# A fused attention and MLP kernel: a decay scan in longer chunks, a smaller first key load, and three transfers and copies put elsewhere

## The chip, the cores and the metric

The kernel runs on one core of a Trainium2 chip. The metric is the device time of one execution in microseconds (us). Before the change it is 359.97 us, the median of three runs (359.89 to 360.4). The profile shows one execution with a span of 358.2 us; all positions in time below are counted from the start of that span.

## The reference

```python
def _attn_ref(q, k, v, s):              # 8 batches, 8 heads, 576 positions, 64 wide
    scores = scale * np.matmul(q, k.transpose(0, 1, 3, 2))
    s_pos = np.maximum(s, 0.0)
    cum = np.cumsum(s_pos, axis=-1)
    bias = -(cum[:, :, :, None] - cum[:, :, None, :])
    scores = np.where(causal, -1000000000.0, scores + np.minimum(bias, 0.0))
    scores = scores - np.max(scores, axis=-1, keepdims=True)
    attn = np.exp(scores)
    attn = attn / (np.sum(attn, axis=-1, keepdims=True) + 1e-09)
    return np.matmul(attn, v)

def _moe_ref(x, w_in, w_out):           # x: 4608 tokens of 512; w_in 512x2048, w_out 2048x512
    h = x @ w_in
    relu6 = np.clip(h + 3.0, 0.0, 6.0)
    return (h * relu6 / 6.0) @ w_out
```

Attention with a decay: each position has a number `s`, its positive part is summed along the sequence, and the difference of two such sums is taken from the score. The result of attention, with the heads side by side, is the input of an MLP with a hardswish between its two matrices.

## The kernel before

**Pairs of heads.** The 64 heads are worked in 32 pairs. A pair has 1152 rows of queries and keys, which are 9 tiles of 128. A tile is cast to f16 and transposed, so that `qT` and `kT` hold 64 rows of head width; four more rows (64 to 67) carry the decay. The running sum enters as three f16 parts of the key (`hi`, `mid`, `lo`, which add up to the f32 value) against rows of ones in the query, and as one negated part in the query against a row of ones in the key. In the other rows up to 127 there is a coarse causal mask. `qkT` has three slots for three pairs in turn.

**Four ways to fill those rows.** The first four pairs (`FIRST = 4`) and the fifth go through `x0`, a tile that lies in the second half of `gT2`: POOL (for a few parts of pair 0 ACT) casts q and k into it, and TensorE transposes its columns of 68 (`turn_first`). The decay columns of these five pairs (`COLS = 5`) are made at the very start by `first_columns`. Pairs 5 to 9 take the decay rows from a scratch tensor in DRAM (`load_aug`); later pairs are transposed by the DMA from `xb`, whose columns 64 to 127 hold mask constants: `load_columns` loads these constants (`xaug`, 288 KB) and `copy_columns` puts them into the two `xb` buffers, once each, on DVE.

**`first_columns`.** `s_first` holds 90 chunks of 64 values of `s`, one chunk to a partition. DVE scans each chunk. TensorE then turns the chunks to columns and adds what the chunks before hold, in f32: for each half of the 128 partitions one matmul with a selection matrix and one with a matrix of "chunks before" (both in `sums`, 63.3 KB of constants). From the result in PSUM DVE makes `hi`, ACT makes the negated column out of `hi`, and DVE makes the rest, `mid` and `lo`.

**Order of the work.** The order in which instructions are written is the order on each engine; there is no scheduler. What matters of it:

- The start: `s_first`, the first parts of q and k of pair 0 and all of pair 1 are put on the queues of SP and ACT; TensorE runs six matmuls on zeros (`keep_warm(6)`), ACT casts, `first_columns` follows, then the first transposes and the first scores. After them comes a loop over the eight heads of pairs 0 to 3, in which the transposes of the next pair stand between the two halves of a head's scores (`scores_half`). `cast_pair(3)` is in the loop at head 3, the transposes of its queries at head 4.
- POOL issues the four quarters of `w_in` (512 KB each as they arrive) at head 4, two before and two after a cast of v, and the four of `w_out` after the loop. A one-row copy out of `w_out_sb` (`fence_dram`) on SP's queue holds the loads of pair 4 back until the third quarter of `w_out` has landed.
- After the loop the MLP of the first 512 tokens begins (`m1`, then `m2`). In between, the decay of all later pairs is computed: `decay_scan`, `decay_rows`, `decay_columns`, and at last on POOL `decay_order`, twelve small copies and one multiplication by -1 into `dec` (L282). Then POOL casts q and k of pair 4 (`cast_pair(FIRST)`), while DVE makes both `copy_columns`. TensorE does four pieces of `m2` and then transposes pair 4.
- `second_pair` works pairs 4 to 8, with the transposes for the next pair and pieces of `m2` in between; after that `weave` mixes attention and MLP by their costs.

Of the kernel before, what the change touches and what calls it, by code (L numbers as in the profile page):

```python
# [9 lines left out]
F32 = mybir.dt.float32  # L10
# [6 lines left out]
def kernel(  # L17
# [48 lines left out]
    def pair_of_banks(b):  # L66
        return PS[:, b:b + 2, :].rearrange("p b c -> p (b c)")

    FIRST = 4
    COLS = FIRST + 1  # L70
    NG = COLS * W2 // 64
    g = np.arange(NG)
    sel_np = g[:, None] == g[None, :]
    low_np = (g[:, None] < g[None, :]) & (g[:, None] // 9 == g[None, :] // 9)
    sums_dram = nc.inline_tensor(
        np.ascontiguousarray(
            np.stack([m[:, k::2] for k in range(2) for m in (sel_np, low_np)], axis=1)
        ).astype(np.float32),
        name="sums",
    )  # L80

# [41 lines left out]
        "p (a t i c) -> p a t i c", a=COLS, t=NTR, i=2  # L123
    )

    s_first = work.tile([NG, 64], F32, tag="s_first", bufs=1)
    sums = work.tile([NG, 4, NG // 2], F32, tag="sums", bufs=1)
    scan = work.tile([NG, 64], F32, tag="scan", bufs=1)
    rest = work.tile([128, NG // 2], F32, tag="rest", bufs=1)
    s_sb = work.tile([NH, SEQ], F32, tag="s0", bufs=1)  # L130
    s8 = work.tile([NH, SEQ], F32, tag="s1", bufs=1)
    c8 = work.tile([NH, SEQ], F32, tag="s2", bufs=1)
# [57 lines left out]
    def mask_rows(sl, i):  # L190
        nc.vector.tensor_copy(out=mask_view(sl, i), in_=mask_view(0, i))
# [11 lines left out]
    def load_part(p, i, t0, t1, eng):  # L203
        b, h0 = (2 * p) // H, (2 * p) % H
        rows = (q, k)[i][b, h0:h0 + 2].rearrange("h s d -> (h s) d")
        eng.dma_start(  # L206
            out=qk_f[p][:, t0:t1, i, :],
            in_=rows.rearrange("(t p) d -> p t d", p=128)[:, t0:t1, :],
        )
# [98 lines left out]
    def transpose_group(p, g):  # L308
        t0, t1 = ((0, 5), (5, 9))[g]
        n = (t1 - t0) * 128  # L310
        pT = f16(PS[:, 3, :], n)
        src = qk_h[p]
        for t in range(t0, t1):
            c = (t - t0) * 128
            transpose_tile(pT[:, c:c + 128], src[:, t, :, :], t == t0, t == t1 - 1)
        sl = p % NS
        c0 = t0 * 128
        for dst, r0 in ((qT, 0), (kT, 64)):
            nc.vector.tensor_copy(out=dst[0:64, sl, c0:c0 + n], in_=pT[r0:r0 + 64, 0:n])  # L319
        if g == 1:  # L320
            qk_h.pop(p)
# [264 lines left out]
    def keep_warm(n):  # L586
        pw = PS[:, 3, :]
        for i in range(n):
            nc.tensor.matmul(
                out=pw, lhsT=warm[:, 0:128], rhs=warm, start=(i == 0), stop=(i == n - 1)  # L590
            )
# [56 lines left out]
    def second_pair(p, fill):  # L648
        s0, s1, v = scores(2 * p), scores(2 * p + 1), values(2 * p)
        first = p == FIRST  # L650

        def more(n=1):
            run(fill[:n])
            del fill[:n]

        load_pair(p + 3)
        run(s0[:1])
        if not first:
            transpose_group(p, 1)
        run(s0[1:2])  # L660
        if not first:
            run(values(2 * p - 1)[0])
        run(s0[2:3])
        if not first:
            run(values(2 * p - 1)[1])
        run(s0[3:])
        cast_qk(p + 1)
        more()
        run(s1[:2])
        if not first:  # L670
            x_transpose(p - 1)
        run(v[0] + s1[2:3] + v[1])
        if not first:
            transpose_group(p + 1, 0)
        run(s1[3:])
        if first:
            transpose_group(p + 1, 0)
        if p + 3 < PTD:
            load_aug(p + 3, nc.sync)
        cast_v(p + 1)  # L680
        if PTD <= p + 2:
            cast_columns(p + 2)
            transpose_dma(p + 2)
        more()
# [57 lines left out]
    def run(tasks):  # L742
        for task, _ in tasks:
            task()

    def first_columns():
        nc.vector.tensor_scalar(
            out=s_first, in0=s_first, scalar1=0.0, scalar2=8.0, op0=ALU.max, op1=ALU.mult
        )
        nc.vector.tensor_tensor_scan(  # L750
            out=scan, data0=s_first, data1=s_first, initial=0.0, op0=ALU.add, op1=ALU.max
        )
        key_rows()
        cT = PS[:, 7, 0:NG // 2]
        for half in range(2):
            o = cT[64 * half:64 * half + 64, :]
            nc.tensor.matmul(
                out=o, lhsT=scan, rhs=sums[:, 2 * half, :], start=True, stop=False
            )
            nc.tensor.matmul(  # L760
                out=o, lhsT=scan[:, 63:64].to_broadcast([NG, 64]), rhs=sums[:, 2 * half + 1, :],
                start=False, stop=True,
            )
        c3 = cT.rearrange("p (a t) -> p a t", a=COLS)
        r3 = rest.rearrange("p (a t) -> p a t", a=COLS)
        hi, mid, lo = (x0[:, :, :, 1, D + j] for j in range(3))
        nc.vector.tensor_copy(out=hi, in_=c3)
        nc.scalar.activation(out=x0[:, :, :, 0, D + 3], in_=hi, func=AF.Copy, scale=-1.0)
        nc.vector.tensor_tensor(out=r3, in0=c3, in1=hi, op=ALU.subtract)
        nc.vector.tensor_copy(out=mid, in_=r3)  # L770
        nc.vector.tensor_tensor(out=lo, in0=r3, in1=mid, op=ALU.subtract)

    def cast_first(p, i, t0, t1, copy):
        copy(out=x0[:, p, t0:t1, i, 0:D], in_=qk_f[p][:, t0:t1, i, :])  # L774

    def turn_first(p, i, t0, t1, b, copy):
        pT = f16(pair_of_banks(b) if (t1 - t0) > 8 else PS[:, b, :], (t1 - t0) * 128)
        for t in range(t0, t1):
            c = (t - t0) * 128
            nc.tensor.matmul(  # L780
                out=pT[0:XW, c:c + 128], lhsT=x0[:, p, t, i, :], rhs=ident,
                is_transpose=True, start=(c % 1024 == 0),
                stop=(t == t1 - 1 or c % 1024 == 896),
            )
        dst = (qT, kT)[i]
        copy(out=dst[0:XW, p % NS, t0 * 128:t1 * 128], in_=pT[0:XW, :])  # L786
# [1 line left out]
    V, A, G = nc.vector, nc.scalar, nc.gpsimd  # L788

    qk_tile(0)  # L790
    nc.sync.dma_start(out=s_first, in_=s.rearrange("b h (c t) -> (b h c) t", t=64)[0:NG])
    load_part(0, 0, 0, 5, A)
    A.dma_start(out=sums, in_=sums_dram.ap())
    load_part(0, 1, 0, 5, nc.sync)
    load_part(0, 0, 5, 9, nc.sync)
    load_part(0, 1, 5, 9, nc.sync)
    nc.scalar.preload_act_table_set("natural_log_exp_and_others")
    load_qk(1, nc.sync)
    load_v(0, nc.sync)
# [2 lines left out]

    keep_warm(6)
    cast_first(0, 0, 0, 5, A.copy)
    cast_first(0, 1, 0, 5, A.copy)
    first_columns()
    keep_warm(2)
    turn_first(0, 0, 0, 5, 4, A.copy)
    turn_first(0, 1, 0, 5, 5, V.tensor_copy)
    cast_first(0, 0, 5, 9, G.tensor_copy)  # L810
    cast_first(0, 1, 5, 9, G.tensor_copy)
    for i in range(2):
        mask_rows(1, i)
    keep_warm(1)
    qk_f.pop(0)

    def cast_pair(p):
        for i in range(2):
            cast_first(p, i, 0, NTR, G.tensor_copy)
        qk_f.pop(p)  # L820

    for hd in range(2 * FIRST):
        p, odd = hd // 2, hd % 2
        scores_half(hd, 0)
        if hd == 0:
            turn_first(0, 0, 5, 9, 6, V.tensor_copy)
            turn_first(0, 1, 5, 9, 7, V.tensor_copy)
        if not odd:
            if p == 0:
                cast_pair(1)  # L830
                more_pads()
            if p == 2:
                for c in range(2):
                    load_w_in(c)
            cast_v(p)
            if p + 1 < FIRST:
                turn_first(p + 1, 0, 0, 9, 4, V.tensor_copy)
            if p == 2:
                for c in range(2, 4):
                    load_w_in(c)  # L840
            if p == 0:
                load_qk(3, nc.sync)
                load_v(2, nc.sync)
            if p == 1:
                load_v(3, nc.sync)
                nc.sync.dma_start(out=s_sb, in_=s.rearrange("b h t -> (b h) t"))
                load_columns()
        elif p + 1 < FIRST:
            turn_first(p + 1, 1, 0, 9, 4, V.tensor_copy)
            if p + 2 < FIRST:  # L850
                cast_pair(p + 2)
        scores_half(hd, 1)
        if hd > 0:
            attend(hd - 1)
        if hd == 1:
            for i in range(2):
                mask_rows(2, i)
        if odd and p > 0:
            x_transpose(p - 1)
# [19 lines left out]
    for p in range(COLS, COLS + 2):  # L879
        load_pair(p)  # L880
        load_aug(p, nc.sync)
    run(m1_0[4:8])
    for i in range(3):
        run(m1_0[8 + 2 * i:10 + 2 * i])
# [4 lines left out]
    cast_pair(FIRST)  # L889
    cast_v(FIRST)  # L890
    fill = m2_of[0]
    for i in range(2):
        copy_columns(i)
    run(fill[:4])
    for g, (t0, t1) in enumerate(((0, 5), (5, 9))):
        for i in range(2):
# [47 lines left out]
```

The softmax here doesn't subtract the row's maximum and nothing guards it: scores larger than these inputs give would overflow.

## Time and profile before

| what | value |
|---|---|
| time, median of 3 | 359.97 us |
| span of the profile | 358.2 us, 7700 instructions |
| PE (TensorE) busy | 349.6 us, 98% |
| ACT, DVE, POOL busy | 208.8, 182.9, 153.3 us |
| bytes moved by DMA | 59.09 MB, mean 165 GB/s |
| first score matmul starts | 8.30 us |
| first matmul of the MLP starts | 25.97 us |

Each line of the timeline gives the start, the length, the engine, the line of the code, the operation, what it writes and reads, how many instructions were merged, and in brackets how long the engine sat idle before and what released it. PEld is the load of TensorE's stationary operand. SPq and ACTq are issues of transfers; the time in such a line is that of the issue, not of the transfer.

### The profile page before, as it was taken

How to read it: one execution, taken by the hardware profiler on the slowest of the kernel's cores; microseconds unless marked ns; L12 is line 12 of the kernel's file. 1: busy time of each engine (PE TensorE's matmuls, PEld its weight loads, DVE VectorE, ACT ScalarE, POOL GpSimd, SP SyncE). 2: the span in 40 equal slices, each digit the busy share in tenths (PEclk: the TensorE clock that was granted, in tenths of full speed). 3: DMA queues.
4: the chain of work that ended last, by engine and by line, in shares of the span. 5: the costliest groups of instructions: out<-in, count | busy, mean ns of one | idle time of the engine just before them, and what ended most of it. 6: DMA issues, size and time to landing. Idle time of an engine off the chain costs nothing.

```text
span 358.2 us, 7700 instructions
## 1 busy us (share of the span) xinstructions
PE 349.6 (98%) x2860; PEld 204.2 (57%) x2860; DVE 182.9 (51%) x314; ACT 208.8 (58%) x391; POOL 153.3 (43%) x378
## 2 busy tenths in 40 slices
PE   7999999999999999999999999999999999999996
PEld 3875557665655555555555555555555544544444
DVE  3758737766534553455435553545255536544531
ACT  3777437668847774677467755776477614533410
POOL 6694377765654444444444554555543200000000
PEclk9999999999999999999999999999999999999999
DMA  8999999999989999999998999999947110000012
GB/s 180 214 193 214 212 228 223 215 208 203 210 180 229 197 197 221 229 210 185 185 249 172 207 204 211 170 208 211 224 87 116 50 59 30 31 30 29 32 59 88
DMA packets 185312, 59.09 MB, mean 165 GB/s; under 512 B 177576, under 2 KB 180050, under 8 KB 185274
## 3 DMA queue, kind: packets, MB, share of 16 engines
q1 hardware_dynamic: 181681, 54.05, 72.0%
q0 software_dynamic: 2688, 4.19, 6.6%
q8 instruction: 22, 0.36, 0.4%
q10 hardware_dynamic: 905, 0.36, 0.4%
q14 instruction: 16, 0.13, 0.1%
HBM read 37.32 MB, written 9.53 MB: 131 GB/s over the span
## 4 chain that ended last, share of the span: by engine, by line
PE 84%; DVE 4%; ACT 3%; DMA 3%; POOL 3%; issue 1%; SPq 1%; POOLq 0%; ACTq 0%; DVEq 0%
PE PS L506 32%; PE PS L549 32%; PE PS L348 10%; PE PS L436 7%; DMA qkf<-in_k_dram 3%; DVE gT L517 2%; ACT trl L516 2%; DVE qkT L319 1%; ACT Pm L356 1%; PE PS L569 1%; PE PS L474 1%; PE PS L304 1%; POOL gT L774 1%; PE PS L414 1%; SPq L206 1%
## 5 line engine op out<-in xcount | busy, mean ns | idle before, releaser
L517 DVE SCALAR_TENSOR_TENSOR gT<-trl,PS 128x512 f16<-128x512 f32 x144 | 98.2, 687 | 103.0 <-ACT trl L516 102.9
L516 ACT ACTIVATE trl<-PS,bias 128x512 f32<-128x512 f32 x144 | 98.8, 692 | 78.3 <-PE PS L506 76.5
L506 PE MATMUL PS<-xT,w_in 128*128 128x512 f16 x576 | 143.2, 380 | 0.8 <-DVE gT L517 0.7
L549 PE MATMUL PS<-w_out_sb,gT 128*128 128x512 f16 x560 | 138.9, 379 | 0.0
L356 ACT ACTIVATE Pm<-PS 128x384 f16<-128x384 f32 x224 | 103.0, 507 | 45.7 <-PE PS L348 44.5
L361 POOL TENSOR_SCALAR_AFFINE_SELECT Pm<-Pm 128x256 f16<-128x256 f16 x224 | 68.4, 307 | 114.1 <-ACT Pm L356 106.3
L506 PEld LDWEIGHTS <-w_in 128*128 128x128 f16 x576 | 61.4, 114 | 45.7 <-issue 2.0
L549 PEld LDWEIGHTS <-gT 128*128 128x128 f16 x560 | 51.4, 98 | 48.2 <-issue 0.3
L348 PE MATMUL PS<-qkT 128*128 128x256 f16 x392 | 63.4, 261 | 0.8 <-DVE qkT L319 0.2
L348 PEld LDWEIGHTS <-qkT 128*128 128x128 f16 x392 | 36.0, 98 | 31.5 <-DVE qkT L319 2.4
L436 PEld LDWEIGHTS <-Pm 128*128 128x128 f16 x960 | 38.7, 97 | 11.0 <-ACT Pm L420 0.4
L436 PE MATMUL PS<-v_h,Pm 128*128 128x65 f16 x960 | 42.3, 194 | 0.6 <-ACT Pm L420 0.3
L558 DVE TENSOR_SCALAR osb<-PS 128x512 f32<-128x512 f32 x35 | 24.1, 688 | 33.9 <-PE PS L549 33.6
L448 DVE TENSOR_TENSOR xs<-PS,r 128x640 f16<-128x640 f32 x32 | 26.4, 824 | 1.1
L286 POOL CAST xb<-qkf 128x1152 f16<-128x1152 f32 x22 | 25.2, 1147 | 0.0
L301 POOL CAST v_h<-v_f 128x640 f16<-128x640 f32 x32 | 23.3, 728 | 0.8 <-DMA v_f<-in_v_dram 0.8
L420 ACT ACTIVATE Pm<-PS 128x896 f16<-128x896 f32 (+1 forms) x16 | 13.1, 836 | 4.5 <-PE PS L414 4.4
L319 DVE COPY qkT<-PS 64x640 f16<-64x640 f16 (+1 forms) x20 | 9.1, 454 | 8.9 <-PE PS L304 8.8
L446 DVE RECIPROCAL r<-PS 128x10 f32<-128x10 f32 x32 | 7.0, 217 | 9.2 <-PE PS L436 9.0
L414 PE MATMUL PS<-qkT 128*128 128x64 f16 (+4 forms) x48 | 9.4, 285 | 0.4 <-DVE qkT L786 0.2
L482 DVE COPY xT<-PS 128x576 f16<-128x576 f16 x14 | 6.4, 455 | 5.7 <-PE PS L474 4.5
L786 DVE COPY qkT<-PS 68x1152 f16<-68x1152 f16 (+2 forms) x13 | 7.2, 585 | 2.9 <-PE PS L780 1.9
(71 smaller groups left out, 119.0 us busy)
## 6 DMA issues: line engine op xcount, KB each, us to landing
out_dram<-osb SPq DMA_DIRECT2D x35, 256.0 KB, 2.7
qkf<-in_q_dram SPq DMA_DIRECT2D x31, 288.0 KB, 3.5
qkf<-in_k_dram SPq DMA_DIRECT2D x31, 288.0 KB, 4.2
v_f<-in_v_dram SPq DMA_DIRECT2D x64, 128.0 KB, 3.8
w_in<-in_moe_w_in_dram POOLq DMA_DIRECT2D x4, 512.0 KB, 9.8
w_out_sb<-in_moe_w_out_dram POOLq DMA_DIRECT2D x4, 512.0 KB, 16.2
v_f<-in_v_dram SPq DMA_DIRECT2D x32, 32.0 KB, 2.8
qkT<-xb SPq DMA_TRANSPOSE x22, 5.1
```

The lines of the kernel that those rows point to most:

```text
L286: nc.gpsimd.tensor_copy(out=x.rearrange("p (i t) c -> p t i c", i=2)[:, :, :, 0:D], in_=qk_f.pop(p))
L301: nc.gpsimd.tensor_copy(out=v_h[:, sl, :, :, 0:D], in_=v_f[:, sl])
L348: nc.tensor.matmul(out=S[:, c:c + hi - lo], lhsT=kT[:, sl, off + 128 * kt:off + 128 * (kt + 1)], rhs=qT[:, sl, off + lo:off + hi], start=( ...
L356: nc.scalar.activation(out=P[:, p0:p0 + n], in_=S[:, 0:n], func=AF.Exp, scale=0.125, bias=0.0)
L361: nc.gpsimd.affine_select(out=view, in_=view, pattern=pattern, compare_op=ALU.is_ge, fill=0.0, base=0, channel_multiplier=-1,)
L436: nc.tensor.matmul(out=O[:, hh, qt * VW:qt * VW + D + 1], lhsT=P[:, c:c + 128], rhs=v_h[:, sl, hh, kt, 0:D + 1], start=(qt == 0), stop=(qt ...
L448: nc.vector.tensor_tensor(out=xs.rearrange("p t h d -> p h t d"), in0=Ov[:, :, :, 0:D], in1=r.to_broadcast([128, 2, 5, D]), op=ALU.mult,)
L506: nc.tensor.matmul(out=ph, lhsT=w_in_t[f // 4][:, kc, f % 4, :], rhs=xT[:, kc, n * 512:(n + 1) * 512], start=(kc == 0), stop=(kc == KC - 1),)
L516: nc.scalar.activation(out=trl, in_=ph, func=AF.Relu, bias=bias3[:, 0:1], scale=1.0)
L517: nc.vector.scalar_tensor_tensor(out=gT2[:, n % 2, f, :], in0=trl, scalar=6.0, in1=ph, op0=ALU.min, op1=ALU.mult)
L549: nc.tensor.matmul(out=po, lhsT=gT2[:, n % 2, f, t4 * 128:(t4 + 1) * 128], rhs=w_out_sb[:, f, :], start=(f == 0), stop=(f == NF - 1),)
L558: nc.vector.tensor_scalar_mul(out=osb, in0=po, scalar1=1.0 / 6.0)
```

## The change

It does eight things. The first five are meant to let the first scores start sooner, the sixth to have the weights of the MLP earlier, the last two to take constants that are needed late out of a busy time:

- `first_columns` works with 30 chunks of 192 values instead of 90 of 64. The constants shrink from 63.3 KB to 14.4 KB (30 x 120 f32). The adding is now one matmul for what lies before and three of 15 columns for the chunk itself, for each half.
- The negated column is read straight from PSUM by ACT, and stands before `hi` instead of after it.
- Of pair 0's keys only three tiles are loaded first, on ACT's queue behind the queries; the other six come on SP's queue in one transfer, after the constants. They are cast by POOL.
- One matmul less keeps TensorE busy after `first_columns` (`keep_warm(1)`).
- The mask rows of slot 1 are copied in two places instead of one, so that DVE comes to pair 0's copies sooner.
- The first quarter of `w_in` is issued between the two casts of pair 3 instead of after both.
- `load_columns` moves from head 2 to behind the loads of pairs 4 to 6.
- `copy_columns` moves from the time of pair 4's casts into `second_pair` for pairs 6 and 7, behind the copies of the next pair's first five transposed tiles.

```diff
-    NG = COLS * W2 // 64
+    CH = SEQ // 3
+    NG = COLS * W2 // CH
+    NC = NG // 2
...
+        if FIRST + 2 <= p < FIRST + 4:
+            copy_columns(p % 2)
         if p + 3 < PTD:
             load_aug(p + 3, nc.sync)
...
             nc.tensor.matmul(
-                out=o, lhsT=scan, rhs=sums[:, 2 * half, :], start=True, stop=False
-            )
-            nc.tensor.matmul(
-                out=o, lhsT=scan[:, 63:64].to_broadcast([NG, 64]), rhs=sums[:, 2 * half + 1, :],
-                start=False, stop=True,
-            )
...
+                out=o, lhsT=scan[:, CH - 1:CH].to_broadcast([NG, 64]),
+                rhs=sums[:, 2 + 3 * half:5 + 3 * half, :].rearrange("g j c -> g (j c)"),
+                start=True, stop=False,
+            )
+            for j, (c, m) in enumerate(blocks[half]):
+                nc.tensor.matmul(
+                    out=o[:, j * NC:(j + 1) * NC],
+                    lhsT=scan[:, 64 * m:64 * m + 64],
+                    rhs=sums[:, c, :],
+                    start=False, stop=(j == 2),
+                )
...
+        nc.scalar.activation(
+            out=x0_of[:, :, :, 0, D + 3], in_=c3, func=AF.Copy, scale=-1.0
+        )
         nc.vector.tensor_copy(out=hi, in_=c3)
-        nc.scalar.activation(out=x0[:, :, :, 0, D + 3], in_=hi, func=AF.Copy, scale=-1.0)
...
-    A.dma_start(out=sums, in_=sums_dram.ap())
-    load_part(0, 1, 0, 5, nc.sync)
+    nc.sync.dma_start(out=sums.rearrange("g m c -> g (m c)"), in_=sums_dram.ap())
+    load_part(0, 1, 0, 3, A)
+    load_part(0, 1, 3, 9, nc.sync)
     load_part(0, 0, 5, 9, nc.sync)
-    load_part(0, 1, 5, 9, nc.sync)
...
-    cast_first(0, 1, 0, 5, A.copy)
+    cast_first(0, 1, 0, 3, A.copy)
     first_columns()
-    keep_warm(2)
+    keep_warm(1)
     turn_first(0, 0, 0, 5, 4, A.copy)
-    turn_first(0, 1, 0, 5, 5, V.tensor_copy)
+    turn_first(0, 1, 0, 3, 5, V.tensor_copy)
+    cast_first(0, 1, 3, 9, G.tensor_copy)
     cast_first(0, 0, 5, 9, G.tensor_copy)
-    cast_first(0, 1, 5, 9, G.tensor_copy)
-    for i in range(2):
-        mask_rows(1, i)
+    mask_rows(1, 1)
...
     def cast_pair(p):
         for i in range(2):
             cast_first(p, i, 0, NTR, G.tensor_copy)
+            if (p, i) == (FIRST - 1, 0):
+                load_w_in(0)
...
         if hd == 0:
+            turn_first(0, 1, 3, 9, 7, V.tensor_copy)
             turn_first(0, 0, 5, 9, 6, V.tensor_copy)
-            turn_first(0, 1, 5, 9, 7, V.tensor_copy)
+            mask_rows(1, 0)
...
             if p == 2:
-                for c in range(2):
-                    load_w_in(c)
+                load_w_in(1)
...
-                load_columns()
...
         load_aug(p, nc.sync)
+    load_columns()
...
-    for i in range(2):
-        copy_columns(i)
```

## The prediction

> **What bounds the kernel now.** I read the page first, then the chain of waits from the start to 50 us, then the timeline of the stages that the change touches.
>
> ```profile
> PE 349.6 (98%) x2860; PEld 204.2 (57%) x2860; DVE 182.9 (51%) x314; ACT 208.8 (58%) x391; POOL 153.3 (43%) x378
> ...
> PE 84%; DVE 4%; ACT 3%; DMA 3%; POOL 3%; issue 1%; SPq 1%; POOLq 0%; ACTq 0%; DVEq 0%
> ```
>
> TensorE is on the chain for 84% of the span. No part of the change takes much work from it, so all that can be won lies in the 16% in which the chain runs elsewhere, and of these only in the stretches that the change touches: the start, the turn to pair 4 at 42 to 48 us, and pairs 6 and 7 at 60 to 72 us.
>
> The chain from 0 to 30 us:
>
> ```profile
> 3.44 5.11 DMA qkf<-in_k_dram
> ...
> 11.65 5.36 DMA qkf<-in_k_dram
> 17.01 0.05 issue
> 17.06 0.68 POOL gT L774
> 17.74 0.04 issue
> 17.77 0.66 PE PS L780 x9
> ```
>
> The start is held by loads of keys, those of pair 1 and then of pair 3: landed at 17.01, cast by POOL, transposed at 17.77. The first five weight loads of a pair's queries wait even for the cast of its keys, since both lie interleaved in `x0`. The first scores are not in this chain:
>
> ```profile
> 4.74 0.46 PE L757 MATMUL PS<-sums,scan 90*64 90x45 f32 x4 [0.75 <-DMA sums<-sums]
> ...
> 5.92 0.40 ACT L768 ACTIVATE gT<-gT 128x45 f16<-128x45 f16 x1 [0.51 <-DVE gT L767]
> ...
> 6.37 1.28 PE L780 MATMUL PS<-idtri,gT 128*68 128x128 f16 x10
> ...
> 8.30 0.61 PE L414 MATMUL PS<-qkT 128*128 128x512 f16 x1 [0.22 <-DVE qkT L786]
> ```
>
> TensorE waited 0.75 us for the constants, and the scores began at 8.30. From there TensorE has nearly no gap until it waits for pair 3 (its row at 17.50 ends 17.72 at the latest; without the wait the transposes would have begun about 0.25 us sooner).
>
> The turn to pair 4, timeline from 42 us:
>
> ```profile
> 43.77 1.10 DVE L248 COPY xb<-xaug 128x1152 f16<-128x1152 f16 x2
> 43.94 1.20 POOL L282 TENSOR_SCALAR dec<-dec 128x288 f16<-128x288 f16 x1
> 45.10 1.27 POOL L774 CAST gT<-qkf 128x576 f16<-128x576 f32 x2
> 46.42 0.14 PEld L780 LDWEIGHTS <-gT 128*68 128x68 f16 x2 [0.30 <-POOL gT L774]
> ```
>
> POOL is the chain here: a multiplication of only 288 elements takes 1.20 us, twice the 0.67 of a cast of 576, beside two DVE copies. TensorE waits 0.30 us for the casts behind it.
>
> [...]
>
> **The change part by part.**
>
> *Start.* DVE's scan grows: 0.19 us for 64 columns and 0.44 for 576 give 0.25 for 192, and 0.31 and 1.35 give 0.57; from 2.74 it ends at about 3.6 instead of 3.3, under the warm-up matmuls that run to 3.99. The constants now come second on SP's queue, 14.4 KB instead of 63.3. They land between 1.9 us after issue (as `s_first` did) and 3.4 (as the constants did), so 3.2 to 4.7; I take 3.5. The adding starts at 4.0 instead of 4.74. It was 4 matmuls in two passes each, 0.60 us from 4.74 to 5.34, 0.075 a pass; now it is 8 matmuls, 16 passes, at most 1.2 us: end 5.2 against 5.4. ACT first casts three key tiles (0.3 us, landing some 4.4 to 5.1), then negates from PSUM: 5.25 to 5.65 instead of 5.92 to 6.32. In the order of the changed program `hi` waits for that ACT instruction, so the four DVE steps, 1.32 us before (5.53 to 6.85), end at about 7.0, later than before. Behind them queue only three transposes of keys instead of five and a copy of 384 columns instead of 640 (0.49 less 256 at 0.5 ns: 0.36). Scores then start at about 7.9, 0.4 sooner; with late keys 8.3.
>
> *What the start is worth.* TensorE would come to pair 3's transposes 0.4 sooner and wait there. These need the keys of pair 3, and up to then the queue is full: at 8 to 17 us it moves 216 GB/s. The 49 KB less are 0.23 us of that. So the gate opens at 17.55 and the start is worth 0.2, whatever the scores gain; 0.45 at most if the keys come sooner, 0 if not.
>
> *`w_in` between the casts.* POOL has 1.68 us idle between the two casts of pair 3 (15.38 to 17.06). The first issue took 0.99 us, so it hides there; the keys' cast is late only if it takes over 1.5. The load landed 8.2 us after its issue at 17.67, that is at 25.9, and the MLP's first matmul began at 25.97: just in time. Started 2 us sooner, in a stretch where the DMA was busy only 0.6 to 0.8, it leaves room for the 0.2. By itself nothing.
>
> *`load_columns` later.* 288 KB leave the stream of weights (1.4 us at 213 GB/s) and `w_in` starts 2 us sooner. The fence, which waited 5.9 us for `w_out` until 40.53, should end at about 37.5, and pairs 4 to 6 come 3 us earlier. No chain before waits for them: the second cast of pair 4 began behind the first, without idle time. Nothing by itself; `xaug` has some 15 us until its first copy.
>
> *`copy_columns` later.* At 43.94 the multiplication meets no copy: 0.3 to 0.5 us instead of 1.20, so the casts end 45.5 to 45.7. TensorE's four pieces of `m2` end at 45.86. The wait of 0.30 goes; I take 0.3. The scores and masks of pair 4 move with it, so the gain stays.
> The two copies, 0.51 and 0.67 us there, now stand on DVE at about 63.5 and 68.7. DVE has a gap of 0.66 us there, but POOL starts its cast of v (0.72) at 63.47, within 0.05 us of the moment at which DVE is free. [...] I take 0.05 each, in the middle 0.1 in all, as the two starts are equal within what the trace resolves.
>
> *Sum:* -0.2 -0.3 +0.1 = -0.4 us; from 359.97, 359.5 to 359.6. I say 359.5.
>
> **The rivals.**
> 1. The start gives more: the keys of pair 3 come 0.45 us sooner and all of the earlier scores count, and with fewer idle gaps TensorE reaches full rate sooner. -0.45 at the start, -0.4 in the middle with copies that cost nothing: 359.1. For it: 0.75 us of wait goes. Against: the full queue.
> [...]
> [...]
>
> **How the numbers follow.** Forecast 0.45, rival 1 0.25, rival 2 0.17, rival 3 0.13. The bound of 0.2% is 0.72 us: below 359.25 lie rival 1 and some of the forecast's good side (0.25 + 0.11), above 360.69 rival 3 and little else (0.14), between them 0.5. The range of 358.7 to 360.5 holds forecast and rival 2 and most of rival 1.
>
> **What would show it.** Right: the adding starts at about 4.0 and the first scores near 7.9; the transposes of pair 3's queries still wait for the keys and start at 17.4 to 17.6; L282's successor takes under 0.6 us and TensorE has no gap at 46; the fence's wait ends by 38; a copy from `xaug` at about 63 beside a longer cast of v. Wrong: the wait at pair 3 gone (rival 1); TensorE idle before the transposes of `xs` in pairs 6 and 7 (rival 2); 512-column matmuls still 0.4 us apart after 10 us, or pair 3's keys landing after 17.1 (rival 3).

## The result and the profile after

The changed kernel takes **361.47 us** (median of six runs, 360.07 to 361.79) against 359.89 for the kernel before on the same chip: ratio **1.0036** with an interval of 1.0019 to 1.0053. The span of its profile is 359.80 us against 358.16: 1.64 us more.

The changed kernel's page, busy times and then the chain by engine:

```profile
PE 351.5 (98%) x2867; PEld 206.3 (57%) x2867; DVE 183.6 (51%) x314; ACT 208.7 (58%) x391; POOL 153.6 (43%) x378
...
PE 78%; DMA 8%; SPq 5%; DVE 3%; ACT 2%; POOL 2%; issue 1%; POOLq 0%; DVEq 0%; ACTq 0%
```

TensorE is busy 1.9 us longer for the same attention and MLP, which is more than the whole loss, so it is not lost to waits. A part is the adding, which takes 1.39 us instead of 0.60 (3.98 to 5.37 below, 4.74 to 5.34 before); for the rest TensorE did the same work more slowly somewhere. Both profiles are of typical executions (361.51 us, and 359.87 before). The timeline of the changed kernel from 3.9 us says where:

```profile
3.98 0.41 PE L763 MATMUL PS<-sums,scan 30*64 30x45 f32 x2
...
4.61 0.82 PE L769 MATMUL PS<-sums,scan 30*64 30x15 f32 x8
...
5.47 0.37 ACT L779 ACTIVATE gT<-PS 128x45 f16<-128x45 f32 x1 [0.31 <-PE PS L769]
5.88 0.36 DVE L782 CAST gT<-PS 128x45 f16<-128x45 f32 x1 [2.04 <-ACT gT L779]
...
6.86 0.53 DVE L785 TENSOR_TENSOR gT<-rest,gT 128x45 f16<-128x45 f32 x1
...
7.45 0.53 PE L794 MATMUL PS<-idtri,gT 128*68 128x128 f16 x3 [0.81 <-DVE gT L785]
...
8.51 0.61 PE L418 MATMUL PS<-qkT 128*128 128x512 f16 x1
...
9.44 2.23 PE L794 MATMUL PS<-idtri,gT 128*68 128x128 f16 x19
...
10.32 0.88 DVE L800 COPY qkT<-PS 68x768 f16<-68x768 f16 x2 [1.39 <-PE PS L794]
...
11.24 0.88 DVE L195 COPY qkT<-qkT 64x1152 f16<-64x1152 f16 x1
11.47 0.64 PE L418 MATMUL PS<-qkT 128*128 128x448 f16 x2
...
12.15 0.75 DVE L800 COPY qkT<-PS 68x1152 f16<-68x1152 f16 x1
...
12.32 0.63 PE L418 MATMUL PS<-qkT 128*128 128x512 f16 x1
...
12.75 0.31 PE L418 MATMUL PS<-idtri 128*128 128x128 f16 x1
...
13.27 0.44 PE L794 MATMUL PS<-idtri,gT 128*68 128x128 f16 x5
```

The same stretch of the kernel before, from the first scores to the same transposes (pair 1's keys, the last row of both fences):

```profile
8.30 0.61 PE L414 MATMUL PS<-qkT 128*128 128x512 f16 x1 [0.22 <-DVE qkT L786]
...
9.11 1.11 PE L780 MATMUL PS<-idtri,gT 128*68 128x128 f16 x17
...
10.06 0.38 PE L414 MATMUL PS<-qkT 128*128 128x448 f16 x2
...
10.69 0.39 PE L414 MATMUL PS<-qkT 128*128 128x512 f16 x1
10.92 0.22 PE L414 MATMUL PS<-idtri 128*128 128x128 f16 x1
...
11.35 0.44 PE L780 MATMUL PS<-idtri,gT 128*68 128x128 f16 x5
```

Read the distance from a 512-column matmul to the next row. Before, it is 0.23 us at 10.69: full rate. After, it is still 0.43 us at 12.32: half rate. The records of the granted rate in the two traces agree: full rate from 8.97 us before, from 13.24 after. (The clock row of the page shows 9 tenths from the first slice on; at the start only the distances tell.)

Pair 1's keys are turned 1.92 us later, and this splits as 0.21 until the first scores, 0.12 until the long row of transposes, 1.08 in that row (19 in 2.03 us instead of 17 in 0.95; two of the 19 stood ahead of the scores before) and 0.51 from there on. A second thing stands in the same stretch on DVE: the mask rows of the queries (L195 at 11.24, 0.88 us) lie between pair 0's last copies and the copy of pair 1's queries (12.15), which TensorE needs before it goes much further. In this execution TensorE did not wait for it: its row at 13.27 has no bracket.

What comes later gained what it was meant to gain. The turn to pair 4, changed kernel:

```profile
45.08 0.69 DVE L521 SCALAR_TENSOR_TENSOR gT<-trl,PS 128x512 f16<-128x512 f32 x1 [0.17 <-ACT trl L520]
45.85 0.94 POOL L286 TENSOR_SCALAR dec<-dec 128x288 f16<-128x288 f16 x1
46.76 1.26 POOL L788 CAST gT<-qkf 128x576 f16<-128x576 f32 x2
...
47.46 0.43 PEld L794 LDWEIGHTS <-gT 128*68 128x68 f16 x5 [0.18 <-POOL gT L788]
47.61 1.38 PE L794 MATMUL PS<-idtri,gT 128*68 128x128 f16 x18
...
48.07 0.76 PEld L794 LDWEIGHTS <-gT 128*68 128x68 f16 x13 [0.18 <-POOL gT L788]
...
48.83 1.03 PE L553 MATMUL PS<-w_out_sb,gT 128*128 128x512 f16 x4
```

The weight loads of the kernel before at the same place:

```profile
45.81 0.31 PEld L780 LDWEIGHTS <-gT 128*68 128x68 f16 x5 [0.45 <-POOL gT L774]
...
46.42 0.76 PEld L780 LDWEIGHTS <-gT 128*68 128x68 f16 x13 [0.30 <-POOL gT L774]
```

Both waits for POOL are shorter, 0.18 us each instead of 0.45 and 0.30; neither is gone. From the last matmul of `m2` ahead of these transposes to the first one behind them it is 1.43 us (47.40 to 48.83) instead of 1.70 (45.48 to 47.18). The fence behind `w_out` stands at 38.09 instead of 40.53, and the casts of v at 65.24 and 70.48, beside the mask copies that stand there now, take 0.93 us instead of 0.72, without a gap on TensorE.

**One number for the end.** The time from the transposes of pair 1's keys to the end of the span is 346.81 us in the kernel before and 346.53 after, and near one of the two in all but two profiles of this case (346.8 without the late moves, 346.5 to 346.6 with them). So the late moves gave 0.28 us, and all of the loss (1.92) lies ahead of 13.3 us. The experiments are read by the same numbers:

| kernel | ratio to before (95%) | first scores | pair 1's keys turned | span | span less keys |
|---|---|---|---|---|---|
| before | | 8.30 | 11.35 | 358.16 | 346.81 |
| after | 1.0036 [1.0019, 1.0053] | 8.51 | 13.27 | 359.80 | 346.53 |
| a_kw2 | 1.0025 [1.0010, 1.0040] | 7.93 | 12.06 | 358.61 | 346.55 |
| a_fill | 1.0010 [1.0002, 1.0019] | 8.57 | 12.58 | 359.14 | 346.56 |
| a_mask | 1.0017 [1.0008, 1.0026] | 8.61 | 12.62 | 359.16 | 346.54 |
| a_mask_fill | 1.0002 [0.9994, 1.0010] | 7.84 | 11.11 | 359.15 | 348.04 |
| a_mask_fill_hi | 1.0005 [0.9996, 1.0013] | 7.86 | 11.82 | 358.39 | 346.57 |
| a_full | 1.0027 [1.0011, 1.0042] | 10.05 | 13.11 | 359.68 | 346.57 |
| a_scan64_mask | 0.9997 [0.9986, 1.0008] | 7.78 | 11.48 | 358.02 | 346.54 |
| b_kw1 | 1.0006 [0.9999, 1.0013] | 8.13 | 11.57 | 358.40 | 346.83 |
| b_mid | 0.9986 [0.9980, 0.9993] | 8.13 | 11.21 | 357.76 | 346.55 |
| b_mid_win | 0.9982 [0.9973, 0.9991] | 8.23 | 11.39 | 357.98 | 346.59 |
| b_scan | 1.0010 [1.0000, 1.0021] | 8.57 | 11.86 | 358.43 | 346.57 |
| b_neg | 1.0020 [1.0011, 1.0028] | 8.56 | 12.57 | 359.10 | 346.53 |
| b_mask | 1.0009 [0.9997, 1.0021] | 8.44 | 11.62 | 358.17 | 346.55 |
| b_keys | 0.9980 [0.9971, 0.9989] | 7.31 | 10.22 | 356.95 | 346.73 |
| b_mid_fill | 1.0001 [0.9991, 1.0011] | 9.18 | 12.06 | 358.63 | 346.57 |
| b_keys_win | 1.0004 [0.9991, 1.0016] | 7.71 | 11.41 | 357.95 | 346.54 |

The times in the last four columns are those of one profiled execution each; the ratios are over all timed executions. Some of the profiled ones were not typical: those of a_kw2 (360.32 us) and b_keys (358.65) are 0.8 to 0.9 us under the medians of their kernels. Two executions far above the rest, 731.36 us of a_scan64_mask and 368.11 us of b_keys_win, are left out of the ratios. The exceptions in the last column are a_mask_fill, explained with its experiment, and b_keys, 0.18 us above b_mid for a reason that stays open.

### The profile page after: what moved, and what is told of

Same layout as the page of the kernel before. It is cut to its first block, busy times and chain, and to the rows that moved or that the text cites. A ratio compares the mean times of both kernels' runs of the same rounds, so it can differ in the third digit from the quotient of the medians.

```text
span 359.8 us, 7714 instructions
## 1 busy us (share of the span) xinstructions
PE 351.5 (98%) x2867; PEld 206.3 (57%) x2867; DVE 183.6 (51%) x314; ACT 208.7 (58%) x391; POOL 153.6 (43%) x378
## 4 chain that ended last, share of the span: by engine, by line
PE 78%; DMA 8%; SPq 5%; DVE 3%; ACT 2%; POOL 2%; issue 1%; POOLq 0%; DVEq 0%; ACTq 0%
PE PS L553 31%; PE PS L510 28%; PE PS L352 10%; PE PS L440 6%; DMA w_out_sb<-in_moe_w_out_dram 4%; DMA v_f<-in_v_dram 2%; SPq L224 2%; SPq L210 2%; DVE gT L521 2%; DMA qkf<-in_k_dram 1%; ACT trl L520 1%; DVE qkT L323 1%; PE PS L573 1%; ACT Pm L360 1%; PE PS L478 1%
## 5 line engine op out<-in xcount | busy, mean ns | idle before, releaser
L521 DVE SCALAR_TENSOR_TENSOR gT<-trl,PS 128x512 f16<-128x512 f32 x144 | 98.2, 686 | 103.0 <-ACT trl L520 102.9
L418 PE MATMUL PS<-qkT 128*128 128x64 f16 (+4 forms) x48 | 10.3, 305 | 0.3 <-ACT Pm L424 0.2
L800 DVE COPY qkT<-PS 68x1152 f16<-68x1152 f16 (+4 forms) x13 | 7.3, 585 | 4.0 <-PE PS L794 3.9
```

The source lines that it names most:

```text
L521: nc.vector.scalar_tensor_tensor(out=gT2[:, n % 2, f, :], in0=trl, scalar=6.0, in1=ph, op0=ALU.min, op1=ALU.mult)
```

## The experiments

Names that begin with a are the changed kernel with something put back or added; names that begin with b are the kernel before with something of the change. Theory A: TensorE stays at half rate too long, because it is idle between the adding and the first scores. Theory B: the order on the other engines makes the start late, and the rate matters little. The four runs under each heading were measured on one chip beside the kernel before, and each heading has another chip.

**Fewer or more keep-warm matmuls, and the late moves alone.**

```diff
 a_kw2:  first_columns()
-        keep_warm(1)
+        keep_warm(2)
 a_fill: turn_first(0, 0, 0, 5, 4, A.copy)
+        keep_warm(2)
         turn_first(0, 1, 0, 3, 5, V.tensor_copy)
 b_kw1:  first_columns()
-        keep_warm(2)
+        keep_warm(1)
 b_mid:  load_columns() behind the loads of pairs 4 to 6,
         copy_columns(p % 2) in second_pair for p = 6, 7, as in the changed kernel
```

> The changed kernel with two keep-warm matmuls after first_columns, as before the change. Theory A (TensorE stays at half rate until 13 us because it is idle too much between the adding and the first scores): one more matmul of 0.43 us fills little of the idle 1.06 us that follows the queries' transposes, so full rate may come at 9 us or still at 13; if it is the removed matmul that decides, the first scores stay near 8.5 but the 19 transposes behind them take about 1.1 us instead of 2.2 and the time is 359.0 to 359.4. Theory B (the start is late because of the order on DVE, ACT and POOL, and the rate matters little): 361.3 to 361.6, unchanged.

> The changed kernel with two more matmuls on zeros between the transposes of pair 0's queries and those of its keys, where TensorE sat idle from 6.6 to 7.45 us. Theory A: full rate by about 9 us or sooner, time 359.0 to 359.4, under the kernel before. Theory B: the matmuls fill idle time and change nothing, 361.3 to 361.6, or 0.1 more.

> The kernel before with one keep-warm matmul after first_columns instead of two, nothing else. Theory A in its narrow form (that matmul decides): full rate at about 12 to 13 us, time 361 to 362. Theory A in its wide form (the longer gap decides, made by the later lo): full rate still near 9 us, 359.9. Theory B: 359.9.

> The kernel before with only the two late parts of the change: mask constants loaded behind the loads of pairs 4 to 6, copies to xb in pairs 6 and 7. Both theories: the wait of TensorE at 46 us goes, 0.3 us less, 359.6; if the copies cost TensorE time in pairs 6 and 7, 359.9 to 360.4.

Measured: 361.13, 360.53, 360.23 and 359.52 us, beside 360.15 of the kernel before. So the late moves are worth 0.14% by themselves, and the start of the changed kernel costs 0.5% against that (1.0036 to 0.9986), 1.8 us. One keep-warm matmul less does little in the kernel before, and one more does little in the changed kernel (1.0025, with an interval that overlaps that of 1.0036). Two matmuls in the gap of 0.81 us take back half of that 0.5%. a_kw2 and a_fill lie between what the two theories gave, so neither is right as it stands. In a_fill another cause comes to light. The timeline of a_fill:

```profile
9.51 1.41 PE L794 MATMUL PS<-idtri,gT 128*68 128x128 f16 x19
10.23 0.88 DVE L800 COPY qkT<-PS 68x768 f16<-68x768 f16 x2 [0.84 <-PE PS L794]
11.14 0.59 DVE L195 COPY qkT<-qkT 64x1152 f16<-64x1152 f16 x1
...
11.77 0.75 DVE L800 COPY qkT<-PS 68x1152 f16<-68x1152 f16 x1
12.58 0.66 PE L794 MATMUL PS<-idtri,gT 128*68 128x128 f16 x9 [0.72 <-DVE qkT L800]
```

Full rate comes at 9.9 us here (19 transposes in 1.41 us instead of 2.23), but the keys of pair 1 then wait 0.72 us for DVE's copy of the queries, and that copy stood behind the mask rows (0.59 us). Two causes lie in parallel, and the later one counts.

**Both repaired, and w_in alone.**

```diff
 a_mask: as the changed kernel, but
-        mask_rows(1, 1)
+        for i in range(2):
+            mask_rows(1, i)
...
-            mask_rows(1, 0)
 a_mask_fill: a_mask, and
         turn_first(0, 0, 0, 5, 4, A.copy)
+        keep_warm(2)
 a_mask_fill_hi: a_mask_fill, and hi ahead of the negation, which reads hi again
 b_mid_win: b_mid, and load_w_in(0) between the two casts of pair 3
```

> The changed kernel, but both mask_rows(1, .) stand together ahead of the loop, as in the kernel before, so that no mask copy lies on DVE between pair 0's copies and the copy of pair 1's queries. Theory A (TensorE at half rate until about 13 us sets the loss): the copies come sooner but TensorE, still at half rate, sets when pair 1's keys are turned; that stays at 13.0 to 13.3 us and the time at 361.0 to 361.5. Theory B (the order on DVE sets the loss): pair 1's keys are turned about 0.7 us sooner, the time falls by 0.6 to 0.8 us to about 360.7, whatever the rate.

> As the kernel before in this list (both mask_rows(1, .) together ahead of the loop), and two keep-warm matmuls between the transposes of pair 0's first queries and first keys. Theory A: no better than the keep-warm matmuls there alone, which gave 360.5. Theory B: the same as with the mask rows moved alone. Both causes in parallel, the later of the two counting: pair 1's keys are turned at about 11.8 to 12.0 us, and the time falls 0.6 to 0.8 us under that of the keep-warm matmuls alone, to 359.7 to 360.0.

> As the one before, and hi ahead of the negation, which reads hi again as in the kernel before, so that the DVE chain hi, mid, lo doesn't wait for ACT. If the later first scores (8.5 instead of 8.3) count: scores at 8.1 to 8.2, another 0.3 to 0.4 us off, 359.3 to 359.6. If they are hidden behind what follows: the same time as the one before within 0.1.

> The kernel before with load_columns and copy_columns late, as in the changed kernel (that alone gave 359.5), and the first quarter of w_in issued between the two casts of pair 3. If the issue hides in POOL's idle time, as predicted: 359.5, within 0.1 of that without it. If it holds back the cast of pair 3's keys, or the load the keys themselves: 359.7 to 359.9. If w_in was what the first matmul of the MLP waited for: 359.2 or less.

Measured: 360.93, 360.23, 360.27 and 359.62 us, beside 360.27. The mask rows alone are worth 0.19% (1.0036 to 1.0017, with intervals that overlap a little), near theory B's 0.6 to 0.8 us. But the two profiles do not show theory B's reason. In that of the changed kernel TensorE did not wait for the copy, and in a_mask it did not either: its 19 transposes take 2.03 us (9.54 to 11.57) as in the changed kernel, and the keys come 0.65 us sooner because full rate was granted at 11.79 us instead of 13.24. The copy counts once the rate is there, as in a_fill and in b_mask below. With the matmuls in the gap as well the loss against the kernel before is gone, but not that against b_mid (0.9986). The expectation of a_mask_fill missed by 0.2 us, and `hi` ahead of the negation gave nothing on top. The load of `w_in` between the casts hides in POOL's idle time, as predicted: no difference from b_mid that the intervals can tell.

The profile of a_mask_fill has the exception of the table: pair 1's keys at 11.11, and yet a span of 359.15. Its timeline, where 1.5 us went:

```profile
95.18 2.79 SPq L297 DMA_TRANSPOSE qkT<-xb  x1
...
101.56 0.34 PE L352 MATMUL PS<-qkT 128*128 128x256 f16 x2 [1.27 <-DMA qkT<-xb]
```

One transposing transfer was issued 2.2 us later than in b_mid (92.94), and its last part landed 6.3 us after the issue instead of 4.8, so TensorE waited. SP's queue issues almost without a pause from 39 to 103 us, so a few slow issues can add up. It is one profile of 18; the cause was not followed.

**What the repaired versions still lacked.** So far the scan in 192, the keys in two other parts and the keep-warm matmuls had not been separated.

```diff
 b_scan: b_mid, and chunks of 192 with their constants and 8 matmuls
-    NG = COLS * W2 // 64
+    NG = COLS * W2 // CH
 b_keys: b_mid, and
-    load_part(0, 1, 0, 5, nc.sync)
+    load_part(0, 1, 0, 3, nc.sync)
+    load_part(0, 1, 3, 9, nc.sync)
     load_part(0, 0, 5, 9, nc.sync)
-    load_part(0, 1, 5, 9, nc.sync)
     (with its casts and transposes in the order of the changed kernel)
 b_mid_fill: b_mid, and keep_warm(2) between the first two turn_first
 a_full: a_mask_fill_hi with keep_warm(4) in both places
```

> The kernel before with the two late moves of the mask columns (359.5 in an earlier group), and the decay scan in chunks of 192 with the smaller constants; loads, keys, the order hi and then negation, and keep-warm matmuls stay as in the kernel before. If the scan itself is harmless: the adding starts 0.6 us sooner and ends about when it did, 359.4 to 359.6. If its many small f32 matmuls are what keeps TensorE at half rate (they count little as work): full rate later than 11 us, 360.2 or more.

> The kernel before with the two late moves, and pair 0's keys in three tiles and six instead of five and four, the second part turned before the rest of the queries, as in the changed kernel; scan, mask rows and keep-warm matmuls as before. If the split is harmless: 359.4 to 359.6. If the smaller first part is what loses (less for TensorE to do at the start, six tiles later on the path): 360.0 to 360.3, and together with the scan it makes up what the repaired versions of the changed kernel (360.2) still lack.

> The kernel before with the two late moves, and two keep-warm matmuls between the first queries' and first keys' transposes. If the rate of TensorE costs time in the kernel before too: full rate by 8 us, 359.0 to 359.3, and a narrower spread. If the keys of pair 3 (landing at 17.0) are what holds the start: 359.5, no change.

> The changed kernel with both mask rows ahead of the loop, hi ahead of the negation, and four keep-warm matmuls after the adding and four between the first transposes, so that TensorE has next to no idle time between 4 and 7.5 us. If the 0.7 us that the repaired versions still lack against the kernel before with the two late moves is half rate in some executions: it goes, 359.4 to 359.6. If it is something else (keys in two parts, transfers later on): still 360.1 to 360.3.

Measured: 360.25, 359.52, 360.24 and 361.29 us, beside 359.95. The scan alone costs 0.24% (0.9986 to 1.0010, 0.9 us): it is the largest idea of the change, and it loses. Its timeline:

```profile
4.16 0.41 PE L763 MATMUL PS<-sums,scan 30*64 30x45 f32 x2 [0.17 <-DMA sums<-sums]
...
4.79 0.82 PE L769 MATMUL PS<-sums,scan 30*64 30x15 f32 x8
5.02 1.15 POOL L158 TENSOR_SCALAR_AFFINE_SELECT qkT<-qkT 64x1152 f16<-64x1152 f16 x1
5.54 1.03 PE L593 MATMUL PS<-warm 128*128 128x512 f16 x2
```

The adding begins 0.4 us sooner than in b_mid (4.58) and takes 1.45 us (4.16 to the end of its last row at 5.61) instead of 0.66 (4.58 to 5.24), so it ends later, and the first scores come at 8.57 instead of 8.13. Full rate came at 10.3 us, not later than 11 as the expectation had it for this loss.

The keys in three and six tiles do no harm. Keep-warm matmuls do, where they stand in the way: at half rate one takes 0.43 us, and in b_mid_fill and a_full the first scores come only at 9.18 and 10.05. Theory A as it was put ("keep TensorE busy and the loss goes") falls with a_full, which was expected at 359.4 to 359.6: full rate was there at 9.1 us, and the path to the first scores was 1.5 us longer than in the changed kernel. b_mid_fill (360.24) and a_full (361.29) missed both of the times that were expected of them.

**The last three parts, and what is left without the two main ones.**

```diff
 b_mask: b_mid, and the mask rows of the queries behind pair 0's last transposes
 b_neg: b_mid, and
+        nc.scalar.activation(out=x0[:, :, :, 0, D + 3], in_=c3, func=AF.Copy, scale=-1.0)
         nc.vector.tensor_copy(out=hi, in_=c3)
-        nc.scalar.activation(out=x0[:, :, :, 0, D + 3], in_=hi, func=AF.Copy, scale=-1.0)
 b_keys_win: b_keys and b_mid_win together
 a_scan64_mask: a_mask, and chunks of 64 with their constants again
```

> The kernel before with the two late moves (359.5), and the mask rows of slot 1 split as in the changed kernel: those of the queries wait until pair 0's last copies are written, and stand on DVE ahead of the copy of pair 1's queries. If this order costs by itself: pair 1's keys are turned 0.6 us later, 360.0 to 360.3. If it costs only beside the late scores of the changed kernel: 359.5 to 359.7.

> The kernel before with the two late moves, and the negation read from PSUM ahead of hi. If hi waits for ACT and this delays the keys' transposes: first scores 0.3 to 0.4 us later (8.4 to 8.6), 359.7 to 359.9. If it is hidden: 359.5.

> The kernel before with what did no harm alone: the two late moves, the keys in three and six tiles, and the first quarter of w_in between the casts. If the parts add: 359.3 to 359.5, faster than either kernel of the case by more than the noise. If w_in and the sooner start get in each other's way: 359.5 to 359.8.

> The changed kernel without what is held to be its two main losses: chunks of 64 and their constants again (on SP's queue), and both mask rows ahead of the loop. If these two are nearly all of the loss: 359.4 to 359.8. If the fewer keep-warm matmuls and the negation ahead of hi matter as much: 360.2 or more.

Measured: 360.38, 360.91, 359.93 and 359.94 us, beside 360.15. Each of three edits loses alone, against b_mid's 0.9986: the mask rows 0.23%, the scan 0.24%, the negation 0.34%. Their sum, 0.81%, is more than the 0.50% that the whole change loses against b_mid, so they seem to overlap. The changed kernel without scan and mask rows is 0.39% faster than with them and level with the kernel before.

These sizes are rough. The parts that did no harm alone were tried together (b_keys_win), and the ratio of 1.0004 lies above that of b_keys (0.9980) and of b_mid_win (0.9982), by more than the intervals allow. Its median is under that of the kernel before, and three executions of 361.8 to 362.4 us lift the ratio; why was not followed. b_mid itself was not run on this chip, so some 0.2% of each difference against it may belong to the chip. Beside b_keys_win the mask rows and the negation cannot be told from nothing by the intervals (1.0009, 1.0020); that both act stands in their profiles. The negation does not cost everywhere, though: a_scan64_mask (0.9997) has it ahead of `hi` too and is faster than b_neg, with intervals apart. The fastest measured, 0.9980 to 0.9986 of before, are b_keys, b_mid_win and b_mid, and their intervals overlap.

In b_mask full rate came at 8.6 us, and TensorE then waited for DVE's copy behind the mask rows:

```profile
10.80 0.22 PE L414 MATMUL PS<-idtri 128*128 128x128 f16 x1
...
11.62 0.66 PE L782 MATMUL PS<-idtri,gT 128*68 128x128 f16 x9 [0.59 <-DVE qkT L788]
```

The negation was expected to cost 0.2 to 0.4 us and cost 1.2. Its timeline:

```profile
5.39 0.37 ACT L769 ACTIVATE gT<-PS 128x45 f16<-128x45 f32 x1
5.79 0.36 DVE L770 CAST gT<-PS 128x45 f16<-128x45 f32 x1 [2.44 <-ACT gT L769]
...
7.15 0.75 PE L782 MATMUL PS<-idtri,gT 128*68 128x128 f16 x5 [0.36 <-DVE gT L773]
...
8.56 0.61 PE L414 MATMUL PS<-qkT 128*128 128x512 f16 x1 [0.23 <-DVE qkT L788]
9.49 2.02 PE L782 MATMUL PS<-idtri,gT 128*68 128x128 f16 x17
...
12.57 0.44 PE L782 MATMUL PS<-idtri,gT 128*68 128x128 f16 x5
```

`hi` waits for ACT, and the scores come 0.43 us later than in b_mid (8.13). The other 0.93 us come behind them: 17 transposes take 2.02 us instead of 1.23, since full rate comes at 12.0 us instead of 9.3.

**The rate by itself.** b_keys and b_keys_win, measured on two chips, are the same program up to 15 us, and their adding began at 4.28 and 4.41. In the profiled execution of the one, full rate came at 5.4 us, in that of the other at 10.1. The row after the first scores and pair 1's keys, b_keys and then b_keys_win:

```profile
7.81 1.22 PE L782 MATMUL PS<-idtri,gT 128*68 128x128 f16 x19
...
10.22 0.66 PE L782 MATMUL PS<-idtri,gT 128*68 128x128 f16 x9
```

```profile
8.64 1.92 PE L782 MATMUL PS<-idtri,gT 128*68 128x128 f16 x19
...
11.41 0.66 PE L782 MATMUL PS<-idtri,gT 128*68 128x128 f16 x9
```

Pair 1's keys are turned 1.19 us apart, 0.13 of it from the adding. So some 1 us hangs on when the rate is granted, and that moves from one execution to another of the same instructions. That it is also why the timed executions of one kernel spread over 1 to 2 us here (the kernel before: 359.36 to 361.64 in one group) is an estimate from this 1 us.

## Why the prediction was wrong

Forecast 359.5, range to 360.5; measured 361.47. What happened is rival 3, the slower one, which had 0.13: TensorE stayed at half rate for longer, and the sign named for it was there, 512-column matmuls still 0.43 us apart at 12.32. By the steps of the prediction:

- *Turn to pair 4, -0.3*: right in size (346.81 to 346.53 us from pair 1's keys to the end), in part by luck. The wait of 0.30 was to go and fell to 0.18; the wait ahead of it, which the sum did not price, fell from 0.45 to 0.18. The multiplication was to fall to 0.3 to 0.5 us without the copies beside it, which no run shows; it takes 0.94, with no DVE row beside it (L521 ends at 45.77, and DVE's next row starts at 47.81). Before, beside two DVE copies that end at 44.87, it took 1.20 and ended at 45.14, 0.26 us more. It did not stand still until the copies ended: with 0.94 from 44.87 it would have ended at 45.81.
- *The two copies, +0.1*: no run shows the 0.05 us each that the sum took. DVE's mask copies began ahead of the casts of v (65.08 and 65.24, 70.32 and 70.48), the casts became 0.21 us longer (0.93 instead of 0.72), and TensorE lost nothing that shows.
- *`load_columns` and `w_in`, nothing*: right (fence at 38.09; b_mid_win).
- *First scores at 7.9*: wrong, 8.51. The start of the adding was right (3.98), and so was the wait of `hi` for ACT. Mis-sized was what follows. The 16 passes took 1.39 us against a bound of 1.2. `lo`, which was to end at 7.0, ended at 7.39: the negation ended at 5.84 instead of 5.65, and DVE's four steps took 1.51 us (5.88 to 7.39) instead of 1.32. From there to the scores it was 1.12 us instead of 0.9. Scan and negation, which were to bring 0.4 us together, cost 0.4 each on the first scores (b_scan, b_neg).
- *The rate*: the step that failed by most. The sum took over from before that TensorE is at full rate from about 9 us, and left the opposite to a rival because the wait of 0.75 ahead of the adding was to go. The runs show that the later wait, behind the adding, goes with the late grant: in the changed kernel full rate came at 13.24, and 1.08 of the 1.92 us lie in one row of transposes at half rate. With two matmuls in that wait (a_fill) it came at 9.9. No run shows the length of half rate that rival 3 was priced with; measured, full rate came 4.27 us later (13.24 instead of 8.97).
- *The mask rows*: never priced. They stood in the diff, and DVE's order told that 0.5 to 0.9 us of copying would stand ahead of the copy that pair 1's keys wait for. Alone it costs up to 0.23%, and it shows as a wait of 0.59 us where the rate comes soon (b_mask).
- *The gate at 17.55*: there was none. The prediction held that pair 3's transposes wait for the cast of its keys, so that the start could be worth 0.2 at most. In b_keys the cast and the transposes stand like this:

```profile
16.60 0.67 POOL L776 CAST gT<-qkf 128x576 f16<-128x576 f32 x1 [0.46 <-DMA qkf<-in_k_dram]
...
16.64 0.66 PE L782 MATMUL PS<-idtri,gT 128*68 128x128 f16 x9
```

The transposes of the queries begin at 16.64, while the cast of the keys runs until 17.27. The rows of transposes of pair 2's keys and pair 3's queries are 2.50 us apart before (15.27, 17.77), after (17.19, 19.69) and in b_keys (14.14, 16.64): this is TensorE's own pace. In the kernel before, the cast happened to end at 17.73, 0.04 us ahead of the row, and the chain of waits put the row down to it. So the start counts nearly one for one, up and down: pair 1's keys come 0.99 us sooner in b_keys than in b_mid, and the span is 0.81 us shorter. The late keys of pair 3 were one part of their load, too: before, 15 of its 16 parts had landed by 15.81 us, and the last came at 17.01; the sum took a full queue for the reason. A gate would have capped the gain, and it would have swallowed part of the loss too; that is how rival 3 was put at 361.0 and not at 361.5.

The traces show of the grant itself: in a_kw2 full rate was granted from 4.67 to 8.08 us, withdrawn for 3.41 us and granted again at 11.50. In a_mask_fill_hi it was granted from 3.96, withdrawn at 7.37 and granted again at 10.78, the same steps: a 512-column row takes 0.39 us at 4.75 and 0.61 at 7.86, and 19 transposes from 8.80 take 2.18. In the 3.41 us up to the withdrawal TensorE was busy for 65% (a_kw2) and 72% (a_mask_fill_hi) of the time. The first grant lay between 2.7 us (a_mask_fill_hi) and 12 us (changed kernel, 13.24) behind the first matmul at 1.25.

How much work TensorE did ahead of a grant can be read off for stretches of the same 3.41 us. In the changed kernel the stretch from 3.00 to 6.41 was full, 1.45 us of it by the small f32 matmuls of the adding, and brought no grant. The next one, from 6.41 to 9.82, holds the wait of 0.81 and was filled to 73%, and brought none either; the rate came at 13.24. Before, the stretch from 5.56 to 8.97, which ended in the grant, was filled to 93% by f16 matmuls. In b_keys the stretch up to the grant (1.99 to 5.40) was filled to 74% by f16 matmuls, and in b_neg one filled to 80% (5.15 to 8.56) brought none. How much work a grant needs was not shown: these shares overlap, and no run varied the work in one stretch alone.

## What to carry to other kernels

Where TensorE's rate changes during the start, as it did here (at 8.97 us before, at 13.24 after), it is part of the cost of an edit: in b_neg 0.43 us more until the first scores cost 1.2. Keep-warm work fills a gap only where it is shorter than the gap; in the way of the path it costs time itself (b_mid_fill: first scores at 9.18 instead of 8.13), and double at half rate (0.43 us instead of 0.22). A wait in the chain that ends within some 0.05 us of the time at which the engine would come anyway is no proof of a gate: look for the same distance between the same rows elsewhere before capping a gain with it. And order on a helper engine (here one copy of mask rows on DVE) belongs in the sum as much as the matmuls do.

## What the runs showed of the hardware that was not expected

- Fewer columns did not make small f32 matmuls shorter: 8 of 30 rows, six of them with 15 columns, took 1.39 us at half rate, against 0.60 for 4 of 90 rows and 45 columns before, also at half rate.
- The rate was withdrawn again from a TensorE that was far from idle: granted at 4.67 us, half from 8.08, full from 11.50 (a_kw2, where TensorE was busy for 65% of the time from 4.67 to 8.08); granted at 3.96, half from 7.37, full from 10.78 (a_mask_fill_hi, 72% from 3.96 to 7.37).
- 3.41 us that small f32 matmuls (1.45 us) and f16 matmuls filled to 100% brought no grant (changed kernel, 3.00 to 6.41); 3.41 us that f16 matmuls alone filled to 93% ended in one (before, 5.56 to 8.97). That the small f32 matmuls count for less is an estimate from these two.
- POOL's multiplication of 128x288 takes 0.94 us by itself, longer than its cast of 128x576 from f32 (0.65), and 1.20 beside two DVE copies.
